# Decode step of two attention and two GeGLU layers on one core: two adjacent channels of x in one partition

## The chip, the core and the metric

The kernel runs on one core of one Trainium2 chip. The metric is the device time of one execution in microseconds (us); lower is better. The kernel before takes 268.86 us, the median of three runs (267.55, 268.86 and 269.77). Engines are named as in the profile: PE (TensorE matmul) with PEld (its weight loads), DVE (VectorE), ACT (ScalarE), POOL (GpSimd), and SP (SyncE), which here only issues DMAs.

## What is computed

Four layers follow each other on x of shape 4 x 1 x 512 (batch 4, one token, 512 channels): attention, feed-forward, attention, feed-forward. Both attentions share one set of weights and caches, and so do both feed-forwards.

```python
def _A_ref(x, k_cache, v_cache, wq, wo):        # 32 query heads, 8 key/value heads, 4096 keys, 128 wide
    q = (x @ wq).reshape(B, Sq, Hq, Dh).transpose(0, 2, 1, 3)
    k, v = jnp.repeat(k_cache, 4, axis=1), jnp.repeat(v_cache, 4, axis=1)
    p = _softmax(jnp.einsum("bhqd,bhkd->bhqk", q, k) * Dh ** -0.5)
    o = jnp.einsum("bhqk,bhkd->bhqd", p, v)
    return o.transpose(0, 2, 1, 3).reshape(B, Sq, Hq * Dh) @ wo
def _B_ref(x, w_gate, w_up, w_down):            # 512 -> 1792 -> 512
    return (_gelu(x @ w_gate) * (x @ w_up)) @ w_down
x = x + _A_ref(_layernorm(x), k_cache, v_cache, wq, wo)
x = x + _B_ref(_layernorm(x), w_gate, w_up, w_down)
x = x + _A_ref(_layernorm(x), k_cache, v_cache, wq, wo)
x = x + _B_ref(_layernorm(x), w_gate, w_up, w_down)
```

All inputs are bf16. The four batch rows don't mix, so the kernel can finish the two layers of one batch row before it starts another.

## The kernel before

**Layout of x.** The 512 channels of x stand in 128 partitions and KD = 4 blocks: `XX` (f32) holds the running x, `xb` (bf16) the copy that PE reads. Channel k*128 + p is in partition p, block k. So every weight matrix that x multiplies has row k*128 + p in partition p, block k (`wq_sb`, `wg_sb`, `wu_sb`), and each product that becomes x again must leave PE in the same order: the output projection takes columns k*128 to k*128 + 127 of `wo_sb` as the weights of block k (`OutProj.heads`, line 395), the down projection likewise of `wd_sb` (`down`, line 486).

**Order of work.** The caches of one batch row take 16 MB and are read twice, once for each attention layer. The kernel pairs the second attention of row b with the first attention of row b + 1 (`attend`), so that K tiles and kept V tiles are shared by a schedule that is written out by hand. Row 0 starts alone (`attend_first`, `dense_first`), the last row ends alone (`attend_last`, `dense_last`), and `dense` does the feed-forward of the rows between. All large loads are issued by SP in one fixed order: half of wq, four whole K heads of 1 MB, the other half of wq, K tiles of 512 KB, V; then, after the V tiles of row 0, `load_rest` (lines 158 to 171) issues wo in four DMAs, gate, up, and down in five, followed by the K and V tiles of the next row. A load into a reused buffer waits until its readers are done.

**DMA completions.** The built program counts DMA completions on eight semaphores in turn, so that a load also waits for the load eight places earlier to have landed. (The listing of the built program shows this: the ninth DMA waits on the semaphore of the first.)

**Loads of weights.** `load_wq(g)` (line 156) loads one half of wq's columns as a block of 128 partitions x 4 rows x 2048 columns: each contiguous piece is 4 KB, 512 pieces to the DMA. Gate and up (lines 162 and 163) load as 128 x 4 rows of 1792 columns, contiguous pieces of 3584 B. wo goes in pieces of 1 KB. Down already has two adjacent rows of F in one partition (pieces of 2 KB).

**Streamed products.** For a single row of x the roles are turned (`streamed_part`, line 309): the row of x is the stationary operand, the weight matrix streams past it, and the result, one long row cut over four groups of 32 partitions, is turned by a 32 x 32 DVE transpose. The cut is chosen by `in_turn` (columns in blocks of 32, each block contiguous) or `adjacent` (32 columns at a step of two, then the 32 between them):

```python
def in_turn(w):
    return w.rearrange("p (c j n) -> p j c n", j=QD, n=QS)
def adjacent(w):
    return w.rearrange("p (k j n e) -> p j k e n", j=QD, n=QS, e=2)
```

`ffn_rows` uses `adjacent` for gate and up, because F stands in pairs; `down_rows` and `q_rows` use `in_turn`. `dense_last` loads `wu_sb` as weights at a step of two (`wu_sb[:, k, at + e:at + 2 * P:2]`), line 275 through `mac`.

**The end.** In `dense_last` the final x is put together in rows: `row` (line 1440) adds, with an identity as moving operand, the channels of `xb` and of its rounding rest `xlo` into a PSUM tile `xr` (8 matmuls of 128 columns), and the down product into `yo` (56 matmuls); `xo` is their sum, and four DMAs write it out.

Of the kernel before, what the change touches and what calls it, by code (L numbers as in the profile page):

```python
# [15 lines left out]
P = 128  # L16
# [20 lines left out]
def kernel(  # L37
# [60 lines left out]
          for t in range(NT)]  # L98
    VP = [wts.tile([P, NT, CH, Dh], BF16, name=f"v_t{i}") for i in range(V_SLOTS // NT)]
    slots = [v[:, t] for v in VP for t in range(NT)]  # L100
    wq_dram = A_wq.rearrange("(k p) n -> p k n", p=P)
    wo_dram = A_wo.rearrange("(i p) n -> p i n", p=P)

    XX = state.tile([P, B, KD], FP32, name="XX")
# [33 lines left out]
    def wide(v, width=WIDE):  # L138
        n = v.shape[-1]
        return v.unsqueeze(1).broadcast_to([P, width // n, n])  # L140
# [8 lines left out]
    def cache_tile(cache, b, kvh, t):  # L149
        if whole(b, kvh):  # L150
            return cache[b, kvh].rearrange("(p t c) d -> t p c d", t=NT, p=P)[t]
        return cache[b, kvh].rearrange("(t p c) d -> t p c d", t=NT, p=P)[t]

    def load_wq(g):
        n = HG * Dh
        dq.dma_start(out=wq_sb[g][:], in_=wq_dram[:, :, g * n:(g + 1) * n])

    def load_rest():
        n = Hq // 4
        for i in range(4):  # L160
            dq.dma_start(out=wo_sb[:, i * n:(i + 1) * n], in_=wo_dram[:, i * n:(i + 1) * n])  # L161
        dq.dma_start(out=wg_sb[:], in_=B_w_gate.rearrange("(k p) n -> p k n", p=P))
        dq.dma_start(out=wu_sb[:], in_=B_w_up.rearrange("(k p) n -> p k n", p=P))
        wd_dram = B_w_down.rearrange("(k p e) n -> p k e n", p=P, e=2)
        wd_pairs = wd_sb.rearrange("p (k e) n -> p k e n", e=2)
        for lo, hi in zip(WD_PARTS, WD_PARTS[1:]):
            if hi - lo > 1:
                own = slice(lo // 2, hi // 2)
                dq.dma_start(out=wd_pairs[:, own], in_=wd_dram[:, own])
            else:  # L170
                dq.dma_start(out=wd_sb[:, lo], in_=wd_dram[:, lo // 2, lo % 2])
# [124 lines left out]
    def streamed(name, n, steps, blocks_of=in_turn):  # L296


        full = acc([n, WIDE], name)
        streamed_part(full, steps, range(len(steps)), blocks_of)  # L300
        return full
# [23 lines left out]
        return streamed(name, KF, [(xb[:, k, b:b + 1], w_sb[:, k]) for k in range(KD)], adjacent)  # L325

    def down_rows(H_bf):
        return streamed("y2", KD, [(H_bf[:, c, :1], wd_sb[:, c]) for c in range(KF)])

    def q_tile():  # L330
        return grp.tile([P, HG], BF16, name="q_bf", tag="q_bf", bufs=1)
# [44 lines left out]
    class OutProj:  # L376
# [8 lines left out]
        def heads(self, h0, n):  # L385
            for i in range(h0, h0 + n):
                for k in range(KD):
                    mac(self.full[:, k], wo_sb[:, i, k * P:(k + 1) * P],
                        wide(self.o(i), self.width),
                        self.n == 0 and k == 0, self.n == Hq - 1)  # L390
                self.n += 1

    class RowProj:
# [23 lines left out]
        def onto(self, proj):  # L417
            for x in self.parts:
                for k in range(KD):
                    mac(proj.full[:, k], x[:, k * P:(k + 1) * P], wide(self.pick, proj.width),  # L420
                        False, False)

    def add_x(b0, nb, y):
# [61 lines left out]
    def down(nb, H_bf, whole):  # L485
        y = acc([KD, WIDE], "y2", whole)
        for c in range(KF):
            for k in range(KD):
                mac(y[:, k], wd_sb[:, c, k * P:(k + 1) * P], wide(H_bf[:, c, :]),
                    c == 0 and k == 0, c == KF - 1)  # L490
        return y[:, :, :nb]

# [466 lines left out]
    def attend_first():  # L959

        b, (gx, gy) = 0, first_groups[0]
        prob1 = {}
        keys = Keys(b, (gx, gy))
        kept, own, other, _ = two(b)
        last = one(b)[-1][0]
        vals = Values(1, b, one(b), prob1, dst1(b), keeps=kept,
                      streamed=[h for h in range(Hkv) if h != last],
                      paired=[h for h in range(Hkv) if h // 2 != last // 2])
        ring.extend(1, b, one(b))
        load_wq(gx)  # L970
        keys.load_heads(GH)
        load_wq(gy)
        keys.load(TG)
        ring.pump()
        make_identity(nc, ident_bf[:])
        build_consts()
        xT_ps = ps_sm.tile([P, KD, B], BF16, name="xT_ps", tag="sm")
        for k in range(KD):
            nc.tensor.transpose(xT_ps[:, k, :], x_bf[:B, k * P:(k + 1) * P], ident_bf[:B, :B])
        nc.vector.tensor_copy(out=xb[:, :, :B], in_=xT_ps[:])  # L980
        nc.vector.tensor_copy(out=XX.rearrange("p b k -> p k b"), in_=xT_ps[:])
        rstd1, mr1 = ln_scale(B, stats(0, B))

        def q_first(g):
            q = q_proj(lambda k: xb[:, k, :B + 1], B + 1, g)
            nc.vector.tensor_scalar(out=cs_q[:, g], in0=q[:, :, B], scalar1=float(D), scalar2=None,
                                    op0=ALU.mult)
            t = apart(wd_sb, [HG, B])
            nc.vector.tensor_tensor(out=t, in0=cols(cs_q[:, g], HG, B),
                                    in1=rows(mr1, HG, B), op=ALU.mult)  # L990
            center(q1_bf[:, g], q[:, :, :B], t, rstd1, B)

        q_first(gx)
        q_build(q1_bf[:, gx, :, b])
        sc1 = new_scores()
        for s in range(GH):
            keys.turn(NT)
            for t in range(NT):
                scores_of(sc1, gx, [(s, t)])
        p0 = soft(sc1)  # L1000
        q_first(gy)
        soft_turn(p0)
        q_build(q1_bf[:, gy, :, b])
        pe, den = soft_swap(p0), soft_den(p0)
        keys.turn()
        prob1[gx] = (pe, soft_recip(den))
        keys.turn(3)
        vals.step(2)
        sc1 = new_scores()
        scores(sc1, gy, 0, last_alone)  # L1010
        keys.turn(4)
        vals.step(3)
        scores(sc1, gy, 1, last_alone)
        vals.step(3, hold=True)
        p0 = soft(sc1)
        vals.flush()
        soft_turn(p0)
        prob1[gy] = (soft_swap(p0), soft_recip(soft_den(p0)))
        vals.step(TG)
        assert vals.left() == 0  # L1020
        load_rest()
        scr = Scratch()
        early = Early(b + 1, second_groups[b])
        heads, twice = pairs(one(b)), o1(b)
        summed = RowProj(lambda i: twice(i).broadcast_to([P, 2]))
        for h in heads[:-1]:
            summed.heads(h, hp)
        summed.split(scr.words.bitcast(BF16))
        proj = OutProj(o1(b), 1)
        proj.heads(heads[-1], rep)  # L1030
        summed.onto(proj)
        proj.n = Hq - rep
        proj.heads(heads[-1] + rep, rep)
        ring.extend(2, b, own)
        return proj.y, early, scr
# [336 lines left out]
    def dense_last(y, full, squares):  # L1372
# [63 lines left out]
            nc.tensor.matmul(clear[:], lhsT=zero, rhs=zero, start=True, stop=True,  # L1436
                             skip_group_check=True)

        def row(to, k, lhsT, rhs):
            nc.tensor.matmul(to[k * QS:k * QS + B], lhsT=lhsT, rhs=rhs, start=False, stop=True,  # L1440
                             skip_group_check=True)

        for x in (xb[:], xlo):
            for k in range(KD):
                row(xr, k, x[:, k, :B], ident_bf[:])

        def less(out, x, shift):
            nc.vector.tensor_tensor(out=out, in0=x[:, :, :B], in1=shift, op=ALU.subtract)
# [124 lines left out]
```

## Time and profile before

| | |
|---|---|
| time of the profiled execution | 268.99 us |
| its span, first to last record | 267.2 us |
| runs | 267.55, 268.86, 269.77 us |
| PE, PEld, DVE, ACT busy | 195.1, 114.8, 182.2, 66.0 us |
| read from HBM | 102.50 MB, 384 GB/s over the span |
| mean granted PE clock | 0.866 of full |

Busy times are sums over the whole span and overlap each other. In the part "40 slices" each digit is the busy share of 6.68 us in tenths. The part "chain that ended last" follows the end of the run back from each piece of work to what released it; its shares add up to the span. Line numbers are those of the kernel before.

### The profile page before, as it was taken

To read this page: it belongs to the slowest core of one execution; us is meant where nothing else is said; L and a number is where in the kernel's file an instruction comes from. 1 tells how busy PE (TensorE), PEld (TensorE's weight loads), DVE (VectorE), ACT (ScalarE), POOL (GpSimd) and SP (SyncE) were. 2 spreads that over 40 slices of the span, in tenths; PEclk is the share of its full clock that TensorE was granted. 3 is DMA by queue.
4 is the path that set the end of the run, shared out by engine and by line. 5 is a ranking of instruction groups with operands and counts; after the bars stand their busy time and mean duration, and the time that the engine had idled before them with its cause. 6 is when DMAs were issued, how large, how long until landed. Compare 5 with 4: busy or idle time off the path is not lost.

```text
span 267.2 us, 8596 instructions
## 1 busy us (share of the span) xinstructions
PE 195.1 (73%) x3767; PEld 114.8 (43%) x3775; DVE 182.2 (68%) x448; ACT 66.0 (25%) x136; POOL 3.9 (1%) x10
## 2 busy tenths in 40 slices
PE   1396246544689796989678968787788687888884
PEld 1333123322255453557436245464363354553563
DVE  3385955451335899884776998746769996568773
ACT  1001001100222422032323520304136103044642
POOL 2000000000001000000000000000000000000001
PEclk9998555655597959799999985899999979999999
DMA  7999999999994999999999999999999999999940
GB/s 244 432 416 421 423 429 417 408 385 406 413 412 177 394 416 417 420 417 400 390 414 416 416 419 421 416 415 375 403 418 418 421 415 418 420 405 405 413 160 3
DMA packets 30732, 103.05 MB, mean 386 GB/s; under 512 B 2788, under 2 KB 7144, under 8 KB 29672
## 3 DMA queue, kind: packets, MB, share of 16 engines
q1 hardware_dynamic: 30672, 102.51, 95.7%
q8 instruction: 29, 0.48, 0.6%
q14 instruction: 7, 0.06, 0.1%
q10 hardware_dynamic: 24, 0.01, 0.0%
HBM read 102.50 MB, written 0.00 MB: 384 GB/s over the span
## 4 chain that ended last, share of the span: by engine, by line
DMA 51%; PE 21%; DVE 16%; SPq 6%; ACT 3%; issue 3%; DVEq 0%
DMA v_t<-in_A_v_cache_dram 25%; DMA kp<-in_A_k_cache_dram 8%; DMA kw<-in_A_k_cache_dram 8%; PE sc L592 6%; DMA wu_sb<-in_B_w_up_dram 5%; DMA kw<-in_A_v_cache_dram 4%; SPq L161 4%; DVE kp L537 3%; PE ot L859 3%; DVE kw L537 3%; PE y L275 3%; PE so L791 2%; PE q L309 1%; DVE q L315 1%; DVE qb L360 1%
## 5 line engine op out<-in xcount | busy, mean ns | idle before, releaser
L592 PE MATMUL sc<-kw,qb 128*32 128x512 bf16 x244 | 39.6, 446 | 5.2 <-DVE kw L537 2.2
L592 PE MATMUL sc<-kp,qb 128*32 128x512 bf16 x268 | 40.1, 450 | 1.0 <-DVE kp L537 0.2
L592 PEld LDWEIGHTS <-qb 128*32 128x32 bf16 x512 | 23.1, 104 | 39.6 <-issue 21.4
L537 DVE STREAM_TRANSPOSE kw<-kw 128x1024 f32<-128x1024 f32 x32 | 38.0, 1215 | 0.7 <-DMA kw<-in_A_k_cache_dram 0.6
L537 DVE STREAM_TRANSPOSE kp<-kp 128x1024 f32<-128x1024 f32 x32 | 36.7, 1199 | 0.0
L859 PE MATMUL ot<-pe,v_t 128*128 128x32 bf16 (+1 forms) x896 | 30.0, 184 | 5.6 <-DMA v_t<-in_A_v_cache_dram 2.8
L859 PEld LDWEIGHTS <-v_t 128*128 128x128 bf16 x896 | 27.7, 100 | 13.7 <-issue 7.4
L614 ACT ACTIVATE pe<-sc,nl 128x512 bf16<-128x512 f32 x8 | 5.5, 687 | 85.9 <-DVE pe L611 67.6
L791 PE MATMUL so<-v_t,pe 128*32 128x256 bf16 x304 | 15.0, 319 | 13.6 <-DMA v_t<-in_A_v_cache_dram 11.6
L799 DVE STREAM_TRANSPOSE so<-so 128x512 f32<-128x512 f32 (+1 forms) x23 | 13.8, 599 | 11.1 <-PE so L791 11.1
L791 PEld LDWEIGHTS <-pe 128*32 128x32 bf16 x320 | 9.1, 105 | 19.4 <-issue 12.5
L602 DVE TENSOR_REDUCE pe<-sc 128x1 f32<-128x512 f32 x12 | 8.3, 691 | 9.2 <-PE sc L592 9.1
L405 PE MATMUL yr<-wo_sb,OT_bf 128*2 128x512 bf16 (+1 forms) x120 | 10.7, 425 | 4.9 <-DMA wo_sb<-in_A_wo_dram 4.9
L647 PE MATMUL x<-pe,ident_bf 128*32 128x128 bf16 x192 | 5.4, 233 | 11.8 <-DVE pe L622 11.8
L647 PEld LDWEIGHTS <-ident_bf 128*32 128x32 bf16 x256 | 5.3, 100 | 16.1 <-issue 14.1
L791 PE MATMUL so<-v_t,pl 128*32 128x256 bf16 x192 | 9.4, 275 | 3.3 <-DMA v_t<-in_A_v_cache_dram 3.3
L650 ACT CAST pe<-x 128x512 bf16<-128x512 f32 x12 | 7.0, 586 | 17.4 <-PE x L647 17.4
L275 PE MATMUL q<-xb,wq_sb 128*128 128x5 bf16 (+1 forms) x192 | 5.7, 173 | 6.5 <-DMA wq_sb<-in_A_wq_dram 6.5
L353 PE MATMUL qe<-q_bf,ident_bf 128*32 128x16 bf16 (+1 forms) x272 | 5.7, 176 | 5.6 <-DVE q_bf L335 2.9
L622 DVE STREAM_TRANSPOSE pe<-pe 128x512 bf16<-128x512 bf16 x12 | 8.4, 696 | 1.1 <-ACT pe L614 1.1
L275 PEld LDWEIGHTS <-wo_sb 128*128 128x128 bf16 x160 | 7.6, 101 | 3.3 <-DMA wo_sb<-in_A_wo_dram 2.6
L482 PEld LDWEIGHTS <-ident_bf 128*128 128x128 bf16 x63 | 5.2, 99 | 8.7 <-issue 4.3
(172 smaller groups left out, 255.2 us busy)
## 6 DMA issues: line engine op xcount, KB each, us to landing
v_t<-in_A_v_cache_dram SPq DMA_DIRECT2D x89, 512.0 KB, 8.5
kp<-in_A_k_cache_dram SPq DMA_DIRECT2D x32, 512.0 KB, 9.9
kw<-in_A_k_cache_dram SPq DMA_DIRECT2D x24, 512.0 KB, 9.6
wq_sb<-in_A_wq_dram SPq DMA_DIRECT2D x2, 2048.0 KB, 7.7
kw<-in_A_k_cache_dram SPq DMA_DIRECT2D x4, 1024.0 KB, 11.6
v_t<-in_A_v_cache_dram SPq DMA_DIRECT2D x4, 1024.0 KB, 14.2
wo_sb<-in_A_wo_dram SPq DMA_DIRECT2D x4, 1024.0 KB, 12.0
wq_sb<-in_A_v_cache_dram SPq DMA_DIRECT2D x3, 1024.0 KB, 11.8
```

Source lines behind the costliest of these rows:

```text
L161: dq.dma_start(out=wo_sb[:, i * n:(i + 1) * n], in_=wo_dram[:, i * n:(i + 1) * n])
L275: nc.tensor.matmul(dst, lhsT=lhsT, rhs=rhs, start=first, stop=last, skip_group_check=True)
L405: nc.tensor.matmul(self.rows[j:j + x.shape[1]], lhsT=x, rhs=wo_sb[:, i], start=self.n < QD, stop=True, skip_group_check=True)
L537: nc.vector.transpose(out=words, in_=words)
L592: nc.tensor.matmul(sc[s * QS:(s + 1) * QS], lhsT=qb[:, w0:w0 + 2 * W], rhs=kt[:, :, be // 2, :, be % 2], start=(t == 0 and be == 0), stop= ...
L602: nc.vector.tensor_reduce(out=m, in_=sc.rearrange("p c j -> p (c j)"), axis=AX.X, op=ALU.min if norm else ALU.max)
L622: nc.vector.transpose(out=flat, in_=flat)
L647: nc.tensor.matmul(x[a * QS:(a + 1) * QS, s], lhsT=ident_bf[:, s * QS:(s + 1) * QS], rhs=pT[:, a], start=True, stop=True, skip_group_check ...
L650: nc.scalar.copy(out=pe, in_=x.rearrange("p s t c h -> p (s t c h)"))
L791: nc.tensor.matmul(ps[d, :NW * QS], lhsT=x[:, w:w + NW].rearrange("p c h -> p (c h)"), rhs=v[:, i:i + NW, d], start=first and i == 0, stop ...
L799: nc.vector.transpose(out=flat, in_=flat)
L859: nc.tensor.matmul(self.ot[:, s % 2], lhsT=v[:, i, :], rhs=wide(pe[:, s, t * CH + i, :], self.ot.shape[-1]), start=(done == 0 and i == 0), ...
```

## The change

Channel k*256 + 2*p + e now stands in partition p, block 2*k + e: two adjacent channels share a partition. What follows from it:

- wq: row 2*p + e of a block of 256 rows goes to partition p. The pieces stay 4 KB (half a row); each half of wq is loaded by two DMAs of 1 MB, one for each pair of blocks, instead of one of 2 MB.
- gate and up: the two rows of a partition are adjacent in memory, so a piece is 7168 B, and a matrix has 256 pieces instead of 512. Still one DMA each.
- Output projection, down projection and the transposes of the input read their 128 columns at a step of two (`every_other`). `down_rows` streams with `adjacent`.
- In `dense_last` each block of 128 output channels takes 64 partitions of two blocks of x: `xr` is made of 16 matmuls of 64 columns that write every second column, instead of 8 of 128.

In the built programs PE has 7517 rows instead of 7501 (8 more weight loads and 8 more matmuls, all for `xr`), SP two more DMAs, and DVE, ACT and POOL the same instructions of the same sizes in the same order.

```diff
-    wq_dram = A_wq.rearrange("(k p) n -> p k n", p=P)
+    wq_dram = A_wq.rearrange("(k p e) n -> p k e n", p=P, e=2)
...
+    def by_pairs(w):
+        return w.rearrange("p (k e) n -> p k e n", e=2)
+
+    def every_other(k):
+        lo = k // 2 * 2 * P + k % 2
+        return slice(lo, lo + 2 * P - 1, 2)
+
     def load_wq(g):
         n = HG * Dh
-        dq.dma_start(out=wq_sb[g][:], in_=wq_dram[:, :, g * n:(g + 1) * n])
+        for k in range(KD // 2):
+            dq.dma_start(out=by_pairs(wq_sb[g][:])[:, k], in_=wq_dram[:, k, :, g * n:(g + 1) * n])
...
-        dq.dma_start(out=wg_sb[:], in_=B_w_gate.rearrange("(k p) n -> p k n", p=P))
-        dq.dma_start(out=wu_sb[:], in_=B_w_up.rearrange("(k p) n -> p k n", p=P))
+        dq.dma_start(out=by_pairs(wg_sb[:]),
+                     in_=B_w_gate.rearrange("(k p e) n -> p k e n", p=P, e=2))
+        dq.dma_start(out=by_pairs(wu_sb[:]),
+                     in_=B_w_up.rearrange("(k p e) n -> p k e n", p=P, e=2))
...
-        return streamed("y2", KD, [(H_bf[:, c, :1], wd_sb[:, c]) for c in range(KF)])
+        return streamed("y2", KD, [(H_bf[:, c, :1], wd_sb[:, c]) for c in range(KF)], adjacent)
...
-                    mac(self.full[:, k], wo_sb[:, i, k * P:(k + 1) * P],
+                    mac(self.full[:, k], wo_sb[:, i, every_other(k)],
...
-                    mac(proj.full[:, k], x[:, k * P:(k + 1) * P], wide(self.pick, proj.width),
+                    mac(proj.full[:, k], x[:, every_other(k)], wide(self.pick, proj.width),
...
-                mac(y[:, k], wd_sb[:, c, k * P:(k + 1) * P], wide(H_bf[:, c, :]),
+                mac(y[:, k], wd_sb[:, c, every_other(k)], wide(H_bf[:, c, :]),
...
-            nc.tensor.transpose(xT_ps[:, k, :], x_bf[:B, k * P:(k + 1) * P], ident_bf[:B, :B])
+            nc.tensor.transpose(xT_ps[:, k, :], x_bf[:B, every_other(k)], ident_bf[:B, :B])
...
-        def row(to, k, lhsT, rhs):
-            nc.tensor.matmul(to[k * QS:k * QS + B], lhsT=lhsT, rhs=rhs, start=False, stop=True,
+        def row(to, k, lhsT, rhs, at=slice(0, P)):
+            nc.tensor.matmul(to[k * QS:k * QS + B, at], lhsT=lhsT, rhs=rhs, start=False, stop=True,
                              skip_group_check=True)
 
         for x in (xb[:], xlo):
             for k in range(KD):
-                row(xr, k, x[:, k, :B], ident_bf[:])
+                half = slice(k % 2 * P // 2, (k % 2 + 1) * P // 2)
+                for e in range(2):
+                    row(xr, k, x[:, k // 2 * 2 + e, :B], ident_bf[:, half], slice(e, P, 2))
```

## The prediction

> **What bounds the kernel now.** I read the 40 slices first, then the chain of waits, then stretches of a few us, then single operations that resemble the new ones.
>
> ```profile
> PEclk9998555655597959799999985899999979999999
> DMA  7999999999994999999999999999999999999940
> GB/s 244 432 416 421 423 429 417 408 385 406 413 412 177 394 416 417 420 417 400 390 414 416 416 419 421 416 415 375 403 418 418 421 415 418 420 405 405 413 160 3
> DMA packets 30732, 103.05 MB, mean 386 GB/s; under 512 B 2788, under 2 KB 7144, under 8 KB 29672
> ...
> DMA 51%; PE 21%; DVE 16%; SPq 6%; ACT 3%; issue 3%; DVEq 0%
> ```
>
> The DMA digits are 9 nearly everywhere: the kernel is the time to read 102.5 MB, plus the start, one hole in the thirteenth slice (177 GB/s), and the tail in the last two. Half of the chain that ended last is DMA. So whatever saves work on PE, DVE or ACT inside the nines is worth nothing, and the change has to be priced in bytes per second, in the hole, and in the tail. The packet line tells what a packet is: 7144 - 2788 = 4356 packets are of 512 B to 2 KB, and wo (4096 rows of 1 KB) with the two down loads of single rows (128 rows each) makes 4352. One contiguous piece is one packet.
>
> The same chain in order of time shows what ends before the hole:
>
> ```profile
> 59.84 14.06 DMA wu_sb<-in_B_w_up_dram
> 73.94 0.96 PE u L1323 x16
> 74.92 0.68 DVE u L1325
> ...
> 76.64 1.15 PE y L275 x40
> ```
>
> The up weights land at 73.94 and from there the feed-forward of row 0, the queries and the first scores of row 1 run one after the other until K slots come free and loads start again (SP's next issue is at 83.10). Gate and up are therefore on the path, as part of the stream of loads. The stretches (start:end, sum, busy PE, PEld, DVE, ACT, POOL with counts, clock, DMA share, GB/s) give the rate by size of piece:
>
> ```profile
> 4.00:8.00 4.00, 0.00 (x0) 0.00 (x0) 0.35 (x3) 0.00 (x0) 1.02 (x1) 1.00 1.04 428
> 10.00:17.00 7.00, 4.38 (x42) 2.02 (x39) 5.72 (x9) 0.00 (x0) 0.00 (x0) 1.00 1.01 423
> 54.00:62.00 8.00, 3.28 (x36) 1.37 (x34) 3.54 (x8) 0.00 (x0) 0.00 (x0) 0.50 1.09 386
> 64.00:72.00 8.00, 4.86 (x58) 2.82 (x59) 1.76 (x7) 1.84 (x4) 0.00 (x0) 0.50 1.03 417
> ...
> 81.00:84.00 3.00, 3.00 (x54) 1.59 (x54) 0.71 (x5) 0.00 (x0) 0.00 (x0) 0.64 0.05 22
> ```
>
> By the order of loads these are wq (4 KB pieces), whole K heads (8 KB), wo (1 KB), gate and up (3.5 KB), and the hole, where DMA is idle and PE is busy all of the time.
>
> **The change part by part.**
>
> *Gate and up, 512 pieces of 3584 B to 256 of 7168 B each.* Time of a piece on one of 16 engines is size x 16 / rate: 42.4 ns for 1 KB, 137.5 for 3.5 KB, 309.9 for 8 KB. From 1 to 3.5 KB that is 38.0 ns per KB and 4.4 ns fixed; from 3.5 to 8 KB, 38.3 per KB and 3.4 fixed. A merged pair drops one fixed part. 512 pairs over 16 engines are 32 per engine: 32 x 3.4 to 4.4 = 0.11 to 0.14 us, and I take -0.12. Bounds: 3.67 MB take 8.80 us at 417 GB/s, 8.57 at 428 (the best of the four stretches): -0.23. At the worst, 386, they take 9.51: +0.71. Nearest are 3.5 and 8 KB, between which the new size lies. All of this lies on the path; what comes earlier is up, and with it down and the K tiles behind it, so the hole moves and doesn't shrink.
>
> *wq, the same 4 KB pieces in another order of rows, in two DMAs for each half.* 4.19 MB at 428 are 9.80 us. No row shows this order. Lower bound: nothing gained. Upper: if row pairs go at wo's 386, 10.87 us, +1.07. I take 0: pieces of 4 KB in other layouts (the K and V tiles) keep the slices at 414 to 421. SP gets two more issues, 0.44 and 0.47 us by the two there are, some 0.5 with the gap each. The first moves the K heads' issue from 1.24 to about 1.74, while 2 MB of wq, at 428 GB/s nearly 5 us, still occupy the engines: hidden. The second, with the rotation over eight semaphores, moves the first K tiles: they now wait for the halves of wq and the first heads, one load further back, and may be issued about 2.5 to 5 us later than 3.83. Behind them SP holds only V of row 0. What hides it are the 8 MB of wq and K heads queued ahead, 20 us of transfer; the last tile waits for the second half of wq as it did (24.54), and from there the distance of eight loads is what it was. Without that cover each lost us of DMA would be a us of time. On PE the third weight load of each first projection gets a wait for the second half of wq; the queue behind it needs that half anyway: 0.
>
> *Weights and moving rows at a step of two* (wo, down, the yt corrections, x). Before has both forms:
>
> ```profile
> L275 PEld LDWEIGHTS <-wo_sb x160: 95/98/130, 65.2 to 259.3; 128*128 128x128 bf16 x160
> ...
> L275 PEld LDWEIGHTS <-wu_sb x24: 96/96/100, 261.7 to 262.2; 128*128 128x128 bf16 x24
> ...
> L309 PE MATMUL y<-wd_sb,words x168: 219/219/230, 128.9 to 240.1; 128*32 128x128 bf16 x168
> L309 PE MATMUL q<-wq_sb,xb x112: 376/379/500, 82.9 to 243.5; 128*32 128x512 bf16 x112
> L309 PE MATMUL g<-wg_sb,xb x48: 349/351/366, 125.4 to 236.5; 128*32 128x448 bf16 x48
> ```
>
> The 24 loads of up in the tail read at a step of two and take 96 ns, against 98 for wo at a step of one. The groups pace alike too: 24 matmuls of 176 ns in 0.77 us are (0.77 - 0.176) / 23 = 25.8 ns apart, wo's 16 in 0.55 us 24.9. Moving rows: from 128 to 512 columns at a step of one, 219 to 379 ns, 0.417 a column, would give 352 for 448; gate, at a step of two, has 351. So 0; the 0.9 ns on some 164 loads on the path (56 of down for row 0, 36 at the end of each later row's first or last attention) bounds it at +0.15.
>
> *xr, 16 matmuls of 64 columns for 8 of 128, writing every second column.* The tail:
>
> ```profile
> 262.50 0.23 PE L1440 MATMUL xr<-ident_bf,xb 128*4 128x128 bf16 x4
> 262.56 0.23 PE L1440 MATMUL xr<-ident_bf,wq_sb 128*4 128x128 bf16 x4
> 263.18 0.51 PE L1440 MATMUL yo<-wd_sb,wq_sb 128*4 128x128 bf16 x24 [0.40 <-DVE wq_sb L1460]
> ```
>
> xr ends at 262.79 and PE then waits 0.40 us for DVE. At the 25.8 ns of the up group, 16 of them with 0.22 for the last end at 263.11: hidden, and the ACT copy of xr that follows (0.27) has until 264.24. If this write went at half that pace, they would end at 263.50 and the tail would grow by 0.3. No row of before writes PSUM at a step of two, so the bounds are 0 and +0.4, and I take 0, since no read at that step costs anything. [...]
>
> **Sum.** -0.12 + 0 + 0 + 0: 268.99 becomes 268.87 in the profiled execution, which stood 0.13 above the median of the runs; so 268.7. This is no change: 1% of this kernel is 2.7 us, about what its measurement can tell from no change.
>
> **The rivals.**
>
> 1. *Slower: weights at a step of two load at half pace.* Place: the y groups of wo and of down on line 275 and its successor. Price: 25 ns on each of 164 loads, 4.1 us, 272.8. It decides from 16 ns a load. For it: the change touches every one of them, and of their kind before has only 24. Against: those 24.
> 2. *Slower: pairs of rows are read worse.* wq and gate and up at 386: +1.07 + 0.71, 270.5. For it: wo shows that the stream can lose 10% by its layout alone. Against: wo's pieces are small, and no new piece is.
> 3. *Faster: the hole closes in part.* At 81 to 84 PE is the path at a granted clock of 0.64, at 80 to 81 of 0.50. At full clock the 3.4 us of work around there would be up to 1.7 shorter: 267.0. The change shifts this work by a tenth of a us, so the clock has little reason to change; but the runs spread by 2.2 us, and something in them does this.
> 4. *The rows aren't merged* and gate and up keep their 3584 B: 268.9. Down's pairs, which are written in the same manner, make packets of 2 KB (they aren't among the 4356 small ones), so I hold it unlikely.
>
> **How the numbers follow.** The forecast 0.72, rival 1 0.05, rival 2 0.08, rival 3 0.08, rival 4 0.05, and 0.02 for a slowdown that I don't see. The range: below, rival 3's 267.0 with the rest of the gain on gate and up, 266.9; above, rival 2's 270.5 without its last tenth, 270.4, which also holds the highest run of before (269.77) with xr's bound. Left out are rival 1, half of rival 2, and the runs' own spread. Chances: faster by over 1% (below 266.2) only if rival 3 comes with a fast measurement, 0.05; slower by over 1% 0.07 (rival 1 and the unseen); within 1% 0.88.
>
> **What would show it.** Packets: 512 fewer in all, out of those from 2 to 8 KB, but for some small ones that the two DMAs add. The stretch of gate and up at 420 to 428 GB/s; below 410, rival 2. Up landing 0.1 to 0.3 us earlier against the last wo. Weight loads of wo and down on line 275's successor at 95 to 98 ns, and the down group of row 0 (56 matmuls) in 2.1 us as now; 3.5 would be rival 1. xr done before the first yo, with the wait for DVE still in front of yo. The hole as wide as before, SP's issue after it some 9 us behind the landing of up. The prediction is wrong if the DMA digits show a second hole near the start (SP's order), or if the stream between 90 and 255 us runs at another rate, for which I have no cause.

## The result and the profile after

The changed kernel takes 270.37 us, the median of 21 runs (269.32 to 273.44), against 268.96 us for the kernel before in as many (267.55 to 271.08). The ratio is 1.0062, with a 95% interval of 1.0041 to 1.0083: slower by 1.7 us (1.1 to 2.2). It is estimated from the fast runs alone (of the 21 after, 273.44 was a slow one) and is not the quotient of the two medians, which lie 1.4 us apart. The profiled execution took 271.14 us with a span of 269.3 (268.99 and 267.2 before).

The page of the changed kernel: clock, DMA share and GB/s in 40 slices, the packets, and the shares of the chain that ended last.

```profile
PEclk9999658655589959799999797999999979999998
DMA  6999999999995999999999999999999999999940
GB/s 155 422 424 410 420 427 421 415 386 405 420 407 224 372 416 417 419 416 417 360 411 416 417 420 417 417 416 387 402 417 416 420 416 417 422 388 384 416 156 3
DMA packets 30252, 103.05 MB, mean 383 GB/s; under 512 B 2820, under 2 KB 7176, under 8 KB 29192
...
DMA 65%; PE 20%; DVE 7%; SPq 4%; ACT 2%; issue 2%; DVEq 0%
```

The picture is the same but for its first slice: 155 GB/s where before had 244. A slice is 6.73 us, so 89 GB/s less is 0.60 MB, which a stream of 420 GB/s needs 1.4 us for. The packets came out as forecast: 512 fewer, and 32 small ones more for the two additional DMAs (30732 - 512 + 32 = 30252). So the rows of gate and up are merged, and the loss isn't there.

Stretches of the changed kernel (start:end, sum, busy PE, PEld, DVE, ACT, POOL with counts, clock, DMA share, GB/s):

```profile
2.00:4.00 2.00, 0.85 (x20) 0.69 (x20) 0.76 (x6) 0.61 (x1) 0.00 (x0) 1.00 0.80 178
4.00:8.00 4.00, 0.00 (x0) 0.00 (x0) 0.34 (x3) 0.00 (x0) 1.02 (x1) 1.00 0.93 291
8.00:10.00 2.00, 0.21 (x2) 0.13 (x2) 0.00 (x0) 0.00 (x0) 0.00 (x0) 1.00 1.09 453
64.00:72.00 8.00, 4.09 (x53) 2.50 (x56) 1.62 (x6) 2.17 (x4) 0.00 (x0) 0.50 1.04 425
```

and those of the kernel before that the prediction hasn't shown:

```profile
2.00:4.00 2.00, 0.85 (x20) 0.68 (x20) 0.75 (x6) 0.62 (x1) 0.00 (x0) 1.00 0.83 227
...
8.00:10.00 2.00, 1.52 (x57) 1.52 (x58) 0.00 (x0) 0.00 (x0) 0.00 (x0) 1.00 1.02 434
```

From 2 to 10 us before moved 227 x 2 + 428 x 4 + 434 x 2 = 3.03 MB, after 178 x 2 + 291 x 4 + 453 x 2 = 2.43 MB. Between 4 and 8 us PE, DVE and ACT have little to do and no issue is late, yet wq comes at 291 GB/s instead of 428; in steps of 1 us it is 242, 246, 291 and 385, and then full rate. The DMA share in it is 0.93: the DMA engines aren't idle, they are occupied and move less. By the records of the packets, those of 4 KB take 224 to 243 ns on average in the last three quarters of the first MB, against 159 to 162 ns at the same place before. Gate and up, at 64 to 72, went from 417 to 425.

What that does to the work, from the changed kernel's timeline of the first 12 us (start, us, engine, line, operation, [idle before <- releaser]):

```profile
0.73 1.30 SPq L164 DMA_DIRECT2D wq_sb<-in_A_wq_dram  x2
...
2.08 3.20 SPq L146 DMA_DIRECT2D kw<-in_A_k_cache_dram  x4
...
5.33 1.39 SPq L164 DMA_DIRECT2D wq_sb<-in_A_wq_dram  x2
...
8.12 0.21 PE L285 MATMUL q<-xb,wq_sb 128*128 128x5 bf16 x2 [4.70 <-DMA wq_sb<-in_A_wq_dram]
10.57 1.58 PE L285 MATMUL q<-xb,wq_sb 128*128 128x5 bf16 x53 [2.24 <-DMA wq_sb<-in_A_wq_dram]
```

SP issues the two DMAs back to back and then the four K heads, so there is always work queued. But PE's first projection on the first MB starts at 8.12, and goes on with the second MB at 10.57; before it started on the whole 2 MB at 8.48.

Stretches over the whole stream show that the start is nearly all of it. First the kernel before from 2 to 24 us, then the changed kernel:

```profile
2.00:24.00 22.00, 12.36 (x132) 6.01 (x132) 12.38 (x23) 0.62 (x1) 1.02 (x1) 1.00 1.00 405
...
2.00:24.00 22.00, 11.57 (x132) 5.88 (x132) 11.33 (x21) 0.61 (x1) 1.02 (x1) 1.00 0.98 377
...
24.00:40.00 16.00, 4.83 (x123) 3.83 (x126) 12.13 (x20) 1.67 (x4) 0.00 (x0) 0.65 1.03 421
40.00:60.00 20.00, 11.49 (x186) 6.55 (x179) 8.93 (x25) 2.16 (x5) 0.00 (x0) 0.67 1.03 407
60.00:100.00 40.00, 30.02 (x522) 17.26 (x525) 21.39 (x58) 10.45 (x19) 1.17 (x2) 0.71 0.95 373
100.00:150.00 50.00, 40.96 (x856) 25.12 (x855) 38.07 (x94) 12.88 (x27) 0.00 (x0) 0.94 1.02 409
150.00:200.00 50.00, 39.76 (x764) 22.57 (x763) 37.62 (x93) 12.08 (x25) 0.00 (x0) 0.95 1.02 411
200.00:255.00 55.00, 44.75 (x922) 26.03 (x919) 44.00 (x102) 19.85 (x40) 0.00 (x0) 0.97 1.02 410
```

The same stretches of the kernel before have 405, 424, 404, 369, 411, 410 and 414 GB/s. A difference times its length over 420 GB/s is the time lost: (405 - 377) x 22 / 420 = 1.47 us up to 24 us, and 0.11, -0.14, -0.38, 0.24, -0.12 and 0.52 in the others, which together are 0.2. Where the stream is the bound for the rest of the run, what is missing at the start isn't given back. The chain of waits says so too: the first `so` group on PE (line 791 before, 801 after), which waits for a V tile, starts 1.66 us later.

```profile
37.00 1.07 PE so L791 x13
...
38.66 1.07 PE so L801 x13
```

### The profile page after: what moved, and what is told of

The parts are those of the page before. It is cut to its first block, busy times and chain, and to the rows that moved or that the text cites. A ratio compares the mean times of both kernels' runs of the same rounds, so it can differ in the third digit from the quotient of the medians.

```text
span 269.3 us, 8613 instructions
## 1 busy us (share of the span) xinstructions
PE 192.8 (72%) x3775; PEld 114.0 (42%) x3783; DVE 182.2 (68%) x448; ACT 66.0 (25%) x136; POOL 3.9 (1%) x10
## 2 busy tenths in 40 slices
DMA packets 30252, 103.05 MB, mean 383 GB/s; under 512 B 2820, under 2 KB 7176, under 8 KB 29192
## 4 chain that ended last, share of the span: by engine, by line
DMA 65%; PE 20%; DVE 7%; SPq 4%; ACT 2%; issue 2%; DVEq 0%
DMA v_t<-in_A_v_cache_dram 31%; DMA kw<-in_A_k_cache_dram 15%; DMA kp<-in_A_k_cache_dram 7%; PE sc L602 5%; DMA wg_sb<-in_B_w_gate_dram 5%; DMA kw<-in_A_v_cache_dram 5%; SPq L169 4%; PE y L285 3%; PE ot L869 3%; DMA wq_sb<-in_A_wq_dram 3%; PE so L801 2%; DVE kp L547 1%; PE q L319 1%; DVE q L325 1%; PE u L492 1%
## 5 line engine op out<-in xcount | busy, mean ns | idle before, releaser
L602 PE MATMUL sc<-kp,qb 128*32 128x512 bf16 x268 | 38.0, 414 | 1.1 <-DVE kp L547 0.2
L809 DVE STREAM_TRANSPOSE so<-so 128x512 f32<-128x512 f32 (+1 forms) x23 | 13.8, 600 | 12.8 <-PE so L801 12.8
L285 PEld LDWEIGHTS <-wq_sb 128*128 128x128 bf16 x192 | 5.3, 99 | 9.5 <-DMA wq_sb<-in_A_wq_dram 9.0
```

Source lines behind the costliest of these rows:

```text
L285: nc.tensor.matmul(dst, lhsT=lhsT, rhs=rhs, start=first, stop=last, skip_group_check=True)
L602: nc.tensor.matmul(sc[s * QS:(s + 1) * QS], lhsT=qb[:, w0:w0 + 2 * W], rhs=kt[:, :, be // 2, :, be % 2], start=(t == 0 and be == 0), stop= ...
L809: nc.vector.transpose(out=flat, in_=flat)
```

## The experiments

Each is built from one of the two kernels and compared with the kernel before on the same chip. **Short start** is worked out from each run's stretch of 2 to 24 us as above, (405 - rate) x 22 / 420; **time** is ratio - 1 times the median of before, with the interval.

| run | what is different | GB/s 4-8 us | GB/s 2-24 us | short start, us | ratio | time, us |
|---|---|---|---|---|---|---|
| after | | 291 | 377 | 1.5 | 1.0062 | 1.7 (1.1 to 2.2) |
| e1_split | before, wq halves in two DMAs | 308 | 384 | 1.1 | 1.0077 | 2.1 (1.3 to 2.8) |
| e2_four_rows | before, other order of wq's rows | 428 | 406 | -0.1 | 1.0010 | 0.3 (-0.4 to 0.9) |
| e3_old_wq | after, wq as before | 423 | 403 | 0.1 | 1.0010 | 0.3 (-0.4 to 0.9) |
| e4_head_first | after, one K head ahead | 329 | 390 | 0.8 | 1.0040 | 1.1 (0.5 to 1.7) |
| g1_first_split | before, first half alone split | 309 | 383 | 1.2 | 1.0056 | 1.5 (0.6 to 2.4) |
| g2_second_split | before, second half alone split | 434 | 399 | 0.3 | 1.0016 | 0.4 (-0.6 to 1.4) |
| g3_act_queue | after, second DMA in ACT's queue | 323 | 382 | 1.2 | 1.0088 | 2.4 (1.5 to 3.3) |
| g4_by_partition | before, halves by 64 partitions | 210 | 301 | 5.4 | 1.0476 | 12.8 (11.4 to 14.1) |
| h1_head_between | after, K head between the two | 347 | 387 | 0.9 | 1.0066 | 1.8 (0.9 to 2.6) |
| h2_four_dmas | before, first half in four DMAs | 316 | 386 | 1.0 | 1.0052 | 1.4 (0.6 to 2.2) |
| h3_fours | four channels to a partition | 418 | 404 | 0.1 | 1.0059 | 1.6 (0.8 to 2.4) |
| j1_other_first | e1 with its DMAs in turn | 313 | 385 | 1.0 | 1.0024 | 0.6 (-0.1 to 1.5) |
| j2_heads_first | after, all four K heads ahead | 426 | 394 | 0.6 | 1.0020 | 0.5 (-0.2 to 1.3) |
| j3_split_heads | before, K heads in two DMAs each | 419 | 396 | 0.5 | 1.0013 | 0.3 (-0.4 to 1.1) |
| j4_three_one | before, first half as 3 + 1 blocks | 369 | 395 | 0.5 | 1.0023 | 0.6 (-0.2 to 1.5) |

The short start is that of one profiled execution. Apart from h3, which pays elsewhere, and g4, whose slow loads go on behind 24 us, it lies in or a little under (e1, g3) the interval of the time.

### Which part of the change it is

**e1_split**: the kernel before, with each half of wq in two DMAs of 1 MB, rows as they were.

```diff
-        dq.dma_start(out=wq_sb[g][:], in_=wq_dram[:, :, g * n:(g + 1) * n])
+        for k in range(0, KD, 2):
+            dq.dma_start(out=wq_sb[g][:, k:k + 2], in_=wq_dram[:, k:k + 2, g * n:(g + 1) * n])
```

> The kernel before with one edit: each half of wq is loaded by two DMAs of 1 MB (blocks 0 and 1, then 2 and 3), rows as before. Theory S (the split costs the start: SP and the queue are slower to get going with two DMAs): 280 to 320 GB/s between 4 and 8 us, as after the change (291), and the time 1.2 to 1.7 us above the kernel before. Theory R (the new order of rows costs it: partitions at a pitch of 16 KB, two adjacent rows, read by all engines abreast from a standing start): 420 to 434 GB/s there as in the kernel before (428), and the same time within 0.3 us.

Measured 1.0077 (1.0048 to 1.0106). Its stretch at the start:

```profile
4.00:8.00 4.00, 0.10 (x2) 0.11 (x2) 0.33 (x3) 0.00 (x0) 1.02 (x1) 1.00 0.94 308
```

The split alone, without any other part of the change, makes the slow start and the whole loss of time.

**e2_four_rows**: the kernel before with one DMA for each half as it was, but four adjacent rows of wq in a partition.

```diff
-    wq_dram = A_wq.rearrange("(k p) n -> p k n", p=P)
+    wq_dram = A_wq.rearrange("(p k) n -> p k n", p=P)
```

> The kernel before with one edit: each half of wq is still one DMA of 2 MB, but the four rows of a partition are adjacent in memory (rows 4p to 4p + 3), so queries are computed with rows of wq that belong to other channels. Theory R: below 350 GB/s between 4 and 8 us and 1 to 2 us above the kernel before. Theory S: 420 to 434 GB/s and the same time within 0.3 us.

Measured 1.0010 (0.9986 to 1.0034).

```profile
4.00:8.00 4.00, 0.00 (x0) 0.00 (x0) 0.33 (x3) 0.00 (x0) 1.02 (x1) 1.00 1.04 428
```

The same 428 GB/s as before: this other order of the rows costs nothing that can be measured.

**e3_old_wq**: the changed kernel with `wq_dram` and `load_wq` of before; gate, up, the steps of two and the tail stay changed.

```diff
-    wq_dram = A_wq.rearrange("(k p e) n -> p k e n", p=P, e=2)
+    wq_dram = A_wq.rearrange("(k p) n -> p k n", p=P)
...
-        for k in range(KD // 2):
-            dq.dma_start(out=by_pairs(wq_sb[g][:])[:, k], in_=wq_dram[:, k, :, g * n:(g + 1) * n])
+        dq.dma_start(out=wq_sb[g][:], in_=wq_dram[:, :, g * n:(g + 1) * n])
```

> The kernel after with wq loaded as in the kernel before (one DMA for each half, row k*128 + p in partition p), so queries are computed with rows of wq that belong to other channels; gate, up, the steps of two and the end are those of the change. If the whole loss is in wq's loads (R or S): 0.1 to 0.4 us faster than the kernel before, from pieces of 7168 B, with 428 GB/s between 4 and 8 us. Rival T (something behind the start, the steps of two or the tail, costs too): slower than the kernel before by 0.3 us or more with the start at 428.

Measured 1.0010 (0.9986 to 1.0033). Everything else of the change together is worth nothing that can be measured. Its gate and up run at 425 GB/s from 64 to 72 us, so the small gain of the merge is there, and too small to be seen in the time.

**g1_first_split** and **g2_second_split**: e1 with only the first, or only the second half of wq split (`step = 2 if g == 0 else KD`, and with `g == 1`).

> The kernel before with only the first half of wq in two DMAs of 1 MB (blocks 0 and 1, then 2 and 3), the second half in one. If what costs is the first transfer of the run (too small, B, or of two pieces in a partition, C): 280 to 320 GB/s between 4 and 8 us and 1 to 1.7 us above the kernel before. If it is the number of DMAs that SP issues in the first 7 us (A): the same, since there is one more. Only a cost of the second half's split (D) leaves it at 428 GB/s and at the time of before.

> The kernel before with only the second half of wq, the sixth load of SP, in two DMAs of 1 MB. A: as slow as with the first half split, 280 to 330 GB/s between 4 and 8 us and 1 us or more above the kernel before, for SP issues as many DMAs. B and C: 420 GB/s or more between 4 and 8 us and the time of before within 0.3 us.

Measured 1.0056 (1.0023 to 1.0090) and 1.0016 (0.9978 to 1.0053). The loss belongs to the first half, the first large load of the program. The second half, split, runs at 397 GB/s from 18 to 23 us where before has 420: the dip is there, but smaller, 0.3 us.

### What makes the first DMA slow

**e4_head_first**: the changed kernel with one whole K head issued ahead of wq.

```diff
+        keys.load_heads(1)
         load_wq(gx)
-        keys.load_heads(GH)
+        keys.load_heads(GH - 1)
```

> The kernel after with the first K head loaded ahead of the first half of wq. If wq's pairs of rows are slow only because they are the first thing read (R, from a standing start): the K head runs at full rate, wq behind it at 400 GB/s or more, and 1 to 1.5 us of the loss comes back, 269 to 269.4, unless the later first query takes it again. If the pairs are slow in themselves the 2 MB take as long as after the change, wherever they stand, and the time stays at 270.4. If S: no change either, 270.4.

Measured 1.0040 (1.0017 to 1.0063). By the rates part of the loss is back, a short start of 0.8 us in place of 1.5; the times, 1.1 us (0.5 to 1.7) and 1.7 (1.1 to 2.2), don't tell the two apart. The rate stays low, but later: 329 GB/s from 4 to 8 us and 383 from 8 to 10. In the records of the first wq DMA, the packets of 4 KB take 159 ns (median) in its first half and 267 in its second.

**g3_act_queue**: the second DMA of the first half in ACT's queue, so that SP's queue holds the first alone and then the heads.

```diff
-            dq.dma_start(out=by_pairs(wq_sb[g][:])[:, k], in_=wq_dram[:, k, :, g * n:(g + 1) * n])
+            queue = nc.scalar if g == 0 and k == 1 else dq
+            queue.dma_start(out=by_pairs(wq_sb[g][:])[:, k],
+                            in_=wq_dram[:, k, :, g * n:(g + 1) * n])
```

> The kernel after with the second DMA of the first half of wq issued by ACT instead of SP, so that both are issued at about 0.74 to 1.3 us and the two queues share the 16 engines. If one queue's small first transfer starves the engines (A, B), the other queue fills them: 400 GB/s or more between 4 and 8 us, and 268.5 to 269.2, 1 us or more below the change. If a transfer of two pieces in a partition is slow in itself at the start (C): 290 GB/s and 270.4 as after the change.

Measured 1.0088 (1.0054 to 1.0121), no better. ACT's packets began only at 6.3 us though they were issued by 2; until then the first MB went alone, and was as slow as in the changed kernel (166 GB/s from 2 to 4 us, 178 there). So it isn't that two DMAs on one queue share the engines.

**g4_by_partition**: the two DMAs of a half take 64 partitions each, with all four pieces of a partition.

```diff
-        dq.dma_start(out=wq_sb[g][:], in_=wq_dram[:, :, g * n:(g + 1) * n])
+        for p in range(0, P, P // 2):
+            own = slice(p, p + P // 2)
+            dq.dma_start(out=wq_sb[g][own], in_=wq_dram[own, :, g * n:(g + 1) * n])
```

> The kernel before with each half of wq in two DMAs of 1 MB by partitions: 64 partitions with all four blocks each. A and B: slow as the split by blocks, 280 to 330 GB/s between 4 and 8 us, 1 to 1.7 us above the kernel before. [...]

Measured 1.0476 (1.0426 to 1.0525), and inconclusive for its question, whether the first load is fast with all four pieces of a partition in one DMA:

```profile
4.00:8.00 4.00, 0.00 (x0) 0.00 (x0) 0.32 (x2) 0.00 (x0) 1.02 (x1) 1.00 1.04 210
8.00:10.00 2.00, 0.00 (x0) 0.00 (x0) 0.00 (x0) 0.00 (x0) 0.00 (x0) 1.00 1.06 221
```

The DMAs to 64 partitions ran at about half of before's 428 and 434 GB/s in both stretches, which covers whatever this was to show. The second half of wq is slow too (284 GB/s from 24 to 40 us, 424 before), so the time is more than its short start.

**h1_head_between**: `load_wq(gx, [0])`, one K head, `load_wq(gx, [1])`, the other heads.

> The kernel after with the first K head issued between the two DMAs of the first half of wq. If the first DMA is slow because the next one, of the same kind, is made ready beside it and shares the making of the pieces (N): with a K head of 128 pieces as neighbour the first MB runs at 400 GB/s or more, and the time comes back to 269 or below. If a DMA of two 4 KB pieces in a partition is made ready at only some 55 pieces a us, whatever follows (C): the first MB takes until about 6.9 us as after the change (4 to 8 us at 290 to 340 GB/s), and the time is 269.8 to 270.4.

**h2_four_dmas**: the kernel before with the first half in four DMAs of one block, 512 KB each (`step = 1 if g == 0 else KD`).

> The kernel before with the first half of wq in four DMAs of 512 KB, one piece in each partition. C, if the pace goes with the pieces that a partition has in one DMA: slower than with two pieces, below 250 GB/s between 4 and 8 us, and 2 us or more above the kernel before. N, if it goes with the number of DMAs made ready beside each other: the same or a little slower than with two (280 to 310 GB/s, 1.2 to 2 us above).

Measured 1.0066 (1.0034 to 1.0098) and 1.0052 (1.0023 to 1.0082), with 347 and 316 GB/s from 4 to 8 us. Both theories then held were off: one of what follows in the queue (whole heads of 8 KB pieces right behind the first MB should have brought 400 or more), one of a pace set by the number of pieces (single pieces should have been below 250).

**j1_other_first**: e1 with blocks 2 and 3 first, `for k in (2, 0) if g == 0 else (0, 2)`.

> The kernel before with each half of wq in two DMAs of 1 MB as in the first experiment, but for the first half blocks 2 and 3 ahead of blocks 0 and 1. If the first small DMA of the run is slow whatever it reads (F): 280 to 320 GB/s between 4 and 8 us, 1.1 to 1.7 us above the kernel before. If it is the region of wq (rows 0 to 255) that reads slowly (G): the slow MB comes second, 380 GB/s or more from 4 to 6 us and below 300 from 6 to 9.

**j2_heads_first**: the changed kernel with `keys.load_heads(GH)` ahead of `load_wq(gx)`.

> The kernel after with all four K heads ahead of the first half of wq. F: the four MB of K go at the full rate from the start (their 8 KB pieces need half as many a us), and by the time wq comes its pieces lie ready: 410 GB/s or more between 4 and 8 us and between 12 and 17 us, and the start's 1.2 us come back. The time is then 268.6 to 269.4, if the first query, some 10 us later, has no one waiting for it that DVE's later transposes cannot make up; 271 or more if it has. G: wq's first MB is slow wherever it stands, below 350 GB/s between 12 and 17 us.

**j3_split_heads**: the kernel before with each K head in two DMAs of 512 KB, pieces of 4 KB.

> The kernel before with wq in one DMA for each half and each of the four K heads in two DMAs of 512 KB (4 KB pieces). F (only the first DMA counts): 420 GB/s or more between 4 and 8 us and the time of the kernel before within 0.4 us. If any small DMAs behind the first slow it (H): below 380 GB/s between 4 and 8 us, or between 8 and 17 us where these heads land, and 0.7 us or more above.

**j4_three_one**: the kernel before with the first half in DMAs of three blocks and one, `for own in (slice(0, 3), slice(3, 4)) if g == 0 else (slice(0, KD),)`.

> The kernel before with the first half of wq in two DMAs, three blocks (1.5 MB) and one (512 KB). If the first DMA's number of pieces sets how fast the start goes: with 384 pieces in place of 256 or 512 the loss is about half, 0.4 to 0.8 us and 340 to 400 GB/s between 4 and 8 us. If only one DMA for the whole 2 MB avoids it: 280 to 330 GB/s and 1.1 to 1.7 us above. If three pieces in a partition are enough: 420 GB/s or more and the time of before.

Measured 1.0024 (0.9995 to 1.0054), 1.0020 (0.9992 to 1.0049), 1.0013 (0.9986 to 1.0039) and 1.0023 (0.9994 to 1.0052). These times alone tell nothing from no change; the rates do. With the other rows first the start is as slow (313 against e1's 308), so it isn't that one region of wq reads slowly. With the K heads first:

```profile
12.00:17.00 5.00, 0.22 (x2) 0.13 (x2) 0.00 (x0) 0.00 (x0) 0.00 (x0) 1.00 0.97 354
```

the start is undisturbed (426 from 4 to 8 us) and the dip stands at 12 to 17 us, where wq now arrives (283 from 14 to 16). Theory F had 410 or more there, G less than 350, and what came is close to G: to be first is not what makes the DMA slow, though the dip is smaller behind the heads (283 GB/s over these two us, against 242 and 246 from 4 to 6 us in the changed kernel). The start of j2 says one thing more. Its first DMA is a K head of 1 MB, as many bytes for each partition as the first wq DMA of the changed kernel, but in one piece of 8 KB in place of two of 4 KB, and it isn't slow. So neither the size of a first DMA nor what it holds for each partition explains the loss. The split heads of j3 have their dip right behind the whole first load, against 434 GB/s before in the first of these stretches and 421 in the second:

```profile
8.00:10.00 2.00, 1.35 (x50) 1.36 (x51) 0.00 (x0) 0.00 (x0) 0.00 (x0) 1.00 1.03 348
12.00:17.00 5.00, 3.58 (x13) 1.55 (x15) 5.00 (x6) 0.00 (x0) 0.00 (x0) 1.00 1.03 415
```

The second stretch is the same kind of DMA, 512 KB in pieces of 4 KB, and nearly at full rate: what is slow are the first of them, not each one. And in j4:

```profile
4.00:8.00 4.00, 0.03 (x1) 0.03 (x2) 0.34 (x3) 0.00 (x0) 1.02 (x1) 1.00 1.01 369
```

369 lies between four pieces to a partition in the first DMA (428) and two (308 and 309) or one (316); one piece is no slower than two.

### Steps of four

**h3_fours**: channel 4p + k in partition p, block k. wq stays one DMA for each half, a partition's four rows of gate and of up are one piece of 14336 B, all reads go at a step of four, and `xr` takes 32 matmuls.

```diff
-        lo = k // 2 * 2 * P + k % 2
-        return slice(lo, lo + 2 * P - 1, 2)
+        return slice(k, D, KD)
...
-        dq.dma_start(out=by_pairs(wg_sb[:]),
-                     in_=B_w_gate.rearrange("(k p e) n -> p k e n", p=P, e=2))
+        dq.dma_start(out=wg_sb[:], in_=B_w_gate.rearrange("(p k) n -> p k n", p=P))
```

> The change carried on to four: channel 4p + k in partition p, block k. wq loads again as one DMA of 2 MB for each half (four adjacent rows in a partition), gate and up as one piece of 14336 B in each partition, all 128-column reads go at a step of four, and the final rows are 32 matmuls of 32 columns that write every fourth column. If the split alone is what the change lost: 428 GB/s between 4 and 8 us and 268.2 to 268.8, the time of the kernel before within 0.4 us. If steps of four or 32 strided writes cost: the start is at 428 and the time still 0.5 us or more above it, with the loss in the weight loads of the y groups (above 98 ns) or between the last xr and the first yo.

Measured 1.0059 (1.0029 to 1.0089). Its start is whole (418), so its loss has another place. Its weight loads and moving rows (ns, least, median and most, with first and last start):

```profile
L284 PEld LDWEIGHTS <-wo_sb x160: 111/113/138, 65.5 to 260.9; 128*128 128x128 bf16 x160
...
L284 PEld LDWEIGHTS <-wd_sb x56: 112/118/120, 76.5 to 79.4; 128*128 128x128 bf16 x56
...
L318 PE MATMUL y<-wd_sb,words x168: 272/294/303, 128.8 to 240.4; 128*32 128x128 bf16 x168
```

By the medians at a step of two, 98, 96 and 217 (below), a step of four costs 15 to 22 ns a load and 77 ns on 128 moving columns. In the tail the 56 yo matmuls took 1.12 us instead of 0.95; the 56 down matmuls of row 0, whose weight loads are the slower ones, took 2.03 us (2.10 before, 1.61 in the changed kernel). Where the rest of the 1.6 us lies wasn't taken apart. Its gate and up, with the largest pieces of all, show 417 GB/s from 64 to 72 us, but that figure hangs on the edge of the window, for a packet counts where it starts. From 63 to 72 us h3 has 429, where e3 has 426 and the kernel before 417:

```profile
63.00:72.00 9.00, 5.46 (x66) 2.79 (x59) 1.62 (x6) 2.27 (x4) 0.00 (x0) 0.50 1.03 429
64.00:72.00 8.00, 4.68 (x58) 2.79 (x59) 1.62 (x6) 2.15 (x4) 0.00 (x0) 0.50 0.99 417
```

So this run doesn't tell whether pieces longer than 7 KB gain more.

## Why the prediction was right or wrong

**The step that failed** is wq. The prediction took "the same 4 KB pieces in another order of rows, in two DMAs for each half" at 0, with a bound that came from the order alone; of the two DMAs it priced SP's issue and the later issue of the K tiles, and found both hidden. They are hidden, though the K heads were issued at 2.08 us and not at 1.74. What it didn't ask is whether the first MB itself would come as fast when it is a DMA of its own. It doesn't: 242 to 291 GB/s from 4 to 7 us in place of 418 to 426. By the rates of e1 and of the changed kernel the term is +1.1 to 1.5 us, and since the stream of loads is the bound, it reaches the end: the time is 1.7 us longer (1.1 to 2.2). e1 shows the split to be enough, e2 that another order of the rows costs nothing, e3 that of the rest nothing that can be measured takes part. The rows that were taken for evidence, K and V tiles in slices of 414 to 421 GB/s, are small DMAs in the middle of a long queue; no row of before has one at the start. The prediction had named a second hole near the start, from SP's order, as a sign of being wrong. The first slice did lose, but with the DMA engines busy and nothing issued too late.

**Luck in the number.** The time is within 1% of the kernel before, to which the prediction gave 0.88, and 270.37 lies inside the range of 266.9 to 270.4 by its last 0.03 us. That is luck: the range reaches so far because of rival 2's price, and rival 2 isn't what happened. The forecast itself was a gain of 0.1 us.

**Gate and up**, taken at -0.12: from 417 to 425 GB/s, 3.67 MB gain 0.17 us. Right in sign and about in size, and not to be seen in e3's time. Whether larger pieces gain more is open, by the two windows of h3. The sign of an earlier landing of up can't be read in the changed kernel: there PE waited for gate, multiplied by it at a granted clock of 0.50, and reached up only at 75.82 us.

**Steps of two**, taken at 0. The changed kernel's weight loads and moving rows:

```profile
L285 PEld LDWEIGHTS <-wo_sb x160: 96/98/133, 67.1 to 261.2; 128*128 128x128 bf16 x160
...
L285 PEld LDWEIGHTS <-wd_sb x56: 96/96/99, 77.8 to 80.3; 128*128 128x128 bf16 x56
...
L319 PE MATMUL y<-wd_sb,words x168: 216/217/231, 130.4 to 241.8; 128*32 128x128 bf16 x168
```

98 ns as before for wo, 96 for wd, 217 for 219: right, and rival 1 (half pace, 272.8) is out. The reading from 24 loads of up in the tail carried over to all of them. A step of four is not free: in h3 a weight load takes 113 to 118 ns for 96 to 98, and 128 moving columns 294 for 217.

**xr**, taken at 0 with +0.4 as a bound. The end of the changed kernel:

```profile
264.43 0.29 PE L1450 MATMUL xr<-ident_bf,xb 128*4 128x64 bf16 x8
264.51 0.32 PE L1450 MATMUL xr<-ident_bf,wq_sb 128*4 128x64 bf16 x8
264.90 0.27 ACT L1476 COPY wq_sb<-xr 128x128 f32<-128x128 f32 x1
265.11 0.95 PE L1450 MATMUL yo<-wd_sb,wq_sb 128*4 128x128 bf16 x56 [0.27 <-DVE wq_sb L1472]
```

The 16 take 0.40 us (264.43 to 264.83) where the 8 took 0.29, and PE still waits 0.27 for DVE ahead of yo: hidden, as forecast. The prediction had reckoned 0.61 us for them, from the 25.8 ns between the matmuls of the up group; they start closer together than that. One matmul that writes every second column takes 217 to 247 ns for 64 columns, while those before took 218 for 128, and the tail didn't grow by the 0.3 us of half pace. So a matmul of half the columns took up to 30 ns longer; no run writes 64 columns without a step, so what the step alone costs is not shown.

**The rivals.** Rival 2 named 270.5, nearly what was measured, by another cause: e1 loses as much with the rows in their old order, another order of wq's rows costs nothing in e2, and gate and up became faster. Rival 3, a shorter hole, happened in part in this profile and didn't decide: queries and first scores of row 1 ran at a granted clock of 1.00 (81 to 84 us, 0.64 before), SP's issue after the hole came 8.2 us behind the start of up instead of 9.2, and the stretch of 60 to 100 us has 373 GB/s for 369, 0.4 us, which is less than the start had lost. Rival 4 is out by the packets.

**What stays open** is why such a DMA is slow. Shown: the start is slow when the first 2 MB of wq come in several DMAs of 4 KB pieces (291 to 316 GB/s from 4 to 8 us, 428 in one DMA), and less so with three blocks in the first (369); it isn't the place of the rows, nor their order in e1 and e2; it isn't a second DMA beside it in the queue; it isn't the size of the first DMA or its bytes for each partition, for a K head in pieces of 8 KB is fast there (426); the DMA engines are occupied (a share of 0.93) and their packets take longer (224 to 243 ns for 159 to 162); and a smaller dip appears where the second half of wq (397 for 420) or the K heads (348 for 434) are split, at the first of the split loads. Two theories, of what follows in the queue and of a pace set by the pieces of a partition, each missed a forecast. No version was found that is faster than the kernel before, and e3, the change without the split, can't be told from it. The new rows of wq in one DMA for each half were not tried.

## What to carry to other kernels

When a kernel is bound by its stream of loads, price each DMA that is split by the rate at which its first pieces come, and not only by its pieces, its bytes and its issue: above all at the start of the program, whose loss of 1.5 us nothing later gave back here. Not every small DMA was slow (415 GB/s for later ones of 512 KB in j3); a row from the middle of the stream told nothing of the start. The bytes moved from 2 to 10 us (2.43 MB for 3.03) told this loss, while the run's clock and its hole moved more visibly (1.00 for 0.64 from 81 to 84 us) and mattered less (0.4 us). A step of two over bf16 weights was free on PE (96 to 98 ns a load) and a step of four was not (113 to 118). So two adjacent channels to a partition is as far as this went, and by the rates it bought 0.2 us in this kernel, which no time here shows.

## What the runs showed of the hardware

- A first load of 2 MB in one DMA moved at 428 GB/s from 4 to 8 us (before and e2; 418 to 434 in e3, g2, h3 and j3); the same bytes in the same pieces of 4 KB as two DMAs at 291 to 313 (after, e1, g1, j1), as four at 316 (h2), as three blocks and one at 369 (j4). Each of the two DMAs of the changed kernel has 128 partitions and 1 MiB, and the first of them moved at 242, 246 and 291 GB/s from 4 to 7 us, where the one DMA had 418 to 426; behind other loads it lost less (354 from 12 to 17 us in j2). A first load of 1 MB in pieces of 8 KB moved at 426 (j2, 4 to 8 us).
- Of loads of 512 KB in pieces of 4 KB behind a whole first load, the first moved at 348 GB/s (8 to 10 us in j3) and later ones of the same kind at 415 (12 to 17 us).
- DMAs to 64 partitions ran at 210 and 221 GB/s (g4, 4 to 8 and 8 to 10 us), about half of the 428 and 434 that those to 128 had before.
- A load to ACT's queue that was issued by 2 us had its first packets at 6.3 us, when 0.86 of the 1 MiB on SP's queue had landed.
- Gate and up in pieces of 3584 and 7168 B ran at 417 and 425 GB/s (64 to 72 us); with 14336 B the stretch from 64 has 417 and that from 63 has 429, so longer pieces are not shown to gain or lose.
- 128 x 128 bf16 weight loads took 96 to 98 ns (median) at a step of one or two and 113 to 118 at a step of four; 128 moving columns took 219, 217 and 294 ns.
